# Batch 0 laid out anew in an attention-and-MoE kernel, and two 256-query tiles put into one MoE group

## The chip, the core and the metric

The kernel runs on one core of a Trainium2 chip. TensorE (PE) multiplies matrices into PSUM, VectorE (DVE), ScalarE (ACT) and GpSimd (POOL) work elementwise, and SyncE (SP) issues transfers; SP, ACT and POOL each have a DMA queue of their own. The metric is the device time in microseconds (us), the median of several runs.

## What is computed

The reference is block-sparse attention (4 batches, 8 heads, 768 positions, 64 channels a head) with a gated feed-forward layer behind it; its inputs and its output are float32.

```python
scores = scale * np.matmul(q, k.transpose(0, 1, 3, 2))
mask = np.abs(blk_i - blk_j) <= 1                       # blocks of 32 positions
mask = mask | (blk_i == 0) | (blk_j == 0) | (blk_i == n_blocks - 1) | (blk_j == n_blocks - 1)
for qb in range(n_blocks):
    for kb in sampled_blocks[qb]:                       # 3 for each block of queries
        mask[qb * block:(qb + 1) * block, kb * block:(kb + 1) * block] = True
attn = softmax(np.where(mask, scores, -1e9))
x = (attn @ v) laid out as (3072, 512)
h = x @ w_in                                            # (512, 2048)
out = (h / (1 + np.exp(-beta * h))) @ w_out             # (2048, 512)
```

## The kernel before, in words

**Pairs of heads.** All work is in float16 with float32 sums. The heads are taken two at a time: `seq` has 16 pairs, four a batch. For pair i, `load` (L105) brings k, q and v into a float32 stage, `cast` (L119) writes them as float16 into `kr`, `qr` (`k_rows`, `q_rows`) and `va`, and k and q are turned so that the channels lie on the partitions: `kT` and `qT`. In batch 0 TensorE turns them (`turn_by_pe`, L138: twelve 128x88 transposes for k and twelve for q, then a copy out of PSUM, L145); from batch 1 on the DMA does (`turn_by_dma`, L128). The mask rides along as 24 extra columns of `kr` and `qr` (`mask_columns`, `more_mask_columns`), so that a score matmul has 88 rows and adds a large negative number where nothing may be attended.

**Steps.** `unit` cuts the work of a pair and a tile of 256 or 512 queries into steps. A step is score matmuls (`sc`, L246: four of 256 columns, or two of 512) and one exponential of 128x1024 on ScalarE (`et`, L249). Some steps later come the products with v (`av`, L268: twelve or twenty-four matmuls a head), the division by the sum (`recip`, `xst`, L273 and L274), and the turn of the result into `xt` (`turn_out`: TensorE, `xtp`, L285, or the DMA, L290). There are 144 steps, 36 a batch, numbered x; steps 0 to 11 are the 256-query tile of batch 0, steps 12 to 35 its 512-query tile.

**MoE groups.** When all four pairs of a tile are in `xt`, the tile "arrives" and its feed-forward work is queued: sixteen h steps (`hp`, L307: four matmuls; tanh on ScalarE, `t_sb`, L312; the product `g` on VectorE, L314) and an o step for each half of 128 queries' output (`op`, L326: eight matmuls of 512 columns), with `osb` (L331) and a store at the end. `feed` puts a share of this queue after every step, so that TensorE has it to do while ScalarE exponentiates. The first tile arrives at step 15.

**Order.** The schedule is written by hand: each engine runs its instructions in the order of the code. The loop over x says what is put where: casts of later batches at `cast_at`, loads at `load_at`, the turns of batch 0's pairs 1 to 3 at x = 0, 3 and 6, and the casts and turns of the last four of the six columns of queries of its pairs at x = 8 to 11. All loads and stores are on SP's queue, but for the weights, which GpSimd's queue takes and casts in the transfer.

Of the kernel before, what the change touches and what calls it, by code (L numbers as in the profile page):

```python
# [17 lines left out]
def kernel(  # L18
# [78 lines left out]
    for t in va_tiles:  # L97
        nc.gpsimd.memset(t[:, :, :, D:VW], 1.0)
    for t in k_rows + q_rows:
        nc.gpsimd.memset(t[:, :, :, KR:P], 0.0)  # L100
# [3 lines left out]
    def load(i, name, c0=0, c1=NC, split=False):  # L104
# [27 lines left out]
    def turn_by_pe(i, which, c0, c1, on_act):  # L132
        rows = (k_rows, q_rows)[which][i % NST]
        dst = kq[seq[i]][which]
        for h in range(2):
            tp = mm_pool.tile([P, NC, P], FP16, tag="mm", name="tp")
            for c in range(c0, c1):
                nc.tensor.transpose(out=tp[0:KR, c, :], in_=rows[:, h, c, 0:KR],  # L138
                                    identity=identity)
            o = dst[0:KR, h, c0 * P:c1 * P]  # L140
            i_ = tp[0:KR, c0:c1, :].rearrange("p c s -> p (c s)")
            if on_act is not None and on_act == h:
# [38 lines left out]
    def mask_columns(x, first, on_act):  # L181
# [7 lines left out]
        else:  # L189
# [4 lines left out]
    id16 = persist.tile([NB, NB], FP16, name="id16")  # L194
    nc.vector.tensor_copy(out=id16, in_=ident)
# [3 lines left out]
    mask_blk = persist.tile([NB, NB], FP32, name="mask_blk")  # L199
    nc.vector.tensor_tensor(out=mask_blk, in0=dif, in1=dif, op=ALU.mult)  # L200
    nc.vector.tensor_scalar(out=mask_blk, in0=mask_blk, scalar1=1.5, scalar2=None,
                            op0=ALU.is_le)
    for val in (0.0, float(NB - 1)):
        nc.vector.scalar_tensor_tensor(out=mask_blk, in0=iota_j, scalar=val, in1=mask_blk,
                                       op0=ALU.is_equal, op1=ALU.max)
        nc.vector.scalar_tensor_tensor(
            out=mask_blk, in0=iota_i[:, 0:1].to_broadcast([NB, NB]), scalar=val,
            in1=mask_blk, op0=ALU.is_equal, op1=ALU.max)
    sb_f32 = persist.tile([NB, 3], FP32, name="sb_f32")
    nc.vector.tensor_copy(out=sb_f32, in_=sb_i32)  # L210
    mask_columns(id16, k_rows[0], True)
    keep_warm(9)
    for r in range(3):
        nc.vector.scalar_tensor_tensor(out=mask_blk, in0=iota_j, scalar=sb_f32[:, r:r + 1],
                                       in1=mask_blk, op0=ALU.is_equal, op1=ALU.max)
    mask16 = persist.tile([NB, NB], FP16, name="mask16")
    nc.vector.tensor_scalar(out=mask16, in0=mask_blk, scalar1=1.0, scalar2=-NEG,
                            op0=ALU.subtract, op1=ALU.mult)
# [16 lines left out]
    def unit(b, j, q0, n, group, by_pe):  # L235
# [44 lines left out]
        def turn_out():  # L280
                xst, xt = box["x"], xt_tiles[group]
                if by_pe:
# [4 lines left out]
                    nc.vector.tensor_copy(out=xt[:, j, 0:n],  # L287
                                          in_=xtp[:, 0:nq, :].rearrange("p c s -> p (c s)"))
                else:
                    nc.sync.dma_start_transpose(  # L290
                        out=xt[:, j, 0:n].rearrange("p (c s) -> p c s", s=P),
# [5 lines left out]
    def moe_steps(group, b, q0, n):  # L297
        box = {}

        def h_step(f):  # L300
            def run():
# [3 lines left out]
                hp = mm_pool.tile([P, 512], FP32, tag="mm", name="hp")  # L305
# [13 lines left out]
        def o_step(ts, half):  # L319
            def run():  # L320
# [8 lines left out]
                if half == 1:  # L329
                    osb = work_pool.tile([P, D_MODEL], FP32, tag="osb", name="osb")  # L330
                    nc.vector.tensor_scalar(out=osb, in0=op, scalar1=0.5, scalar2=None,  # L331
                                            op0=ALU.mult)
                    rows = out[b * S:(b + 1) * S, :].rearrange("(p c) m -> c p m", c=NC)
                    nc.sync.dma_start(out=rows[q0 // P + ts], in_=osb)
# [156 lines left out]
```

## Time and profile before

| | |
|---|---|
| median of 3 runs | 311.38 us (309.2 to 312.13) |
| profiled execution | 311.44 us |
| its span, first to last instruction | 309.5 us |
| mean granted TensorE clock | 0.975 |
| busy: PE / ACT / DVE / POOL | 289.8 / 208.6 / 155.8 / 17.6 us |
| moved by DMA | 41.30 MB |

A busy matmul in the profile is not one at its peak, since matmuls are pipelined and their ends are modelled. So the pace of matmuls is read from stretches in which many follow one another.

### The profile page before, as it was taken

Reading aid. Unit: us, or ns where it says so; the run is one execution under the profiler, and the core shown is the slowest. Engines: PE = TensorE matmul, PEld = TensorE weight load, DVE = VectorE, ACT = ScalarE, POOL = GpSimd, SP = SyncE. Lnnn points to the kernel's source line nnn. Section 1 sums busy time; section 2 is a strip of 40 time slices with the busy share of each in tenths; the row PEclk is TensorE's granted clock in tenths of the full one; section 3 lists DMA queues with packets and bytes.
Section 4 is the critical chain, followed back from the end, with each engine's and each line's share of the span. In section 5 each row is a group of like instructions: output and inputs, shape, how many; then the busy total and the mean of one; then the engine's idle time right before and its main releaser. Section 6 shows DMA issues by size and latency. Waiting matters only on the chain.

```text
span 309.5 us, 6342 instructions
## 1 busy us (share of the span) xinstructions
PE 289.8 (94%) x2588; PEld 175.9 (57%) x2588; DVE 155.8 (50%) x383; ACT 208.6 (67%) x277; POOL 17.6 (6%) x40
## 2 busy tenths in 40 slices
PE   7876999889999998999999999999999999999894
PEld 5755576445555554656666656655555565554651
DVE  6765357543576442664426446624554126752551
ACT  3553599757997555996658778868996558850350
POOL 7680000000000000000000000000000000000000
PEclk9995599999999999999999999999999999999999
DMA  5999997996348989303362969551000210001101
GB/s 170 341 257 245 267 185 182 280 230 180 85 153 103 306 223 222 70 10 112 124 208 58 241 132 271 102 128 36 18 19 0 87 53 34 0 2 68 70 0 68
DMA packets 68447, 41.30 MB, mean 133 GB/s; under 512 B 47924, under 2 KB 65348, under 8 KB 68420
## 3 DMA queue, kind: packets, MB, share of 16 engines
q1 hardware_dynamic: 64196, 36.72, 46.5%
q0 software_dynamic: 4224, 4.19, 8.2%
q8 instruction: 20, 0.33, 0.4%
q14 instruction: 7, 0.06, 0.0%
HBM read 27.27 MB, written 6.29 MB: 108 GB/s over the span
## 4 chain that ended last, share of the span: by engine, by line
PE 81%; DVE 8%; ACT 6%; issue 3%; DMA 1%; ACTq 0%; DVEq 0%
PE op L326 27%; PE hp L307 22%; PE sc L246 18%; PE av L268 11%; ACT t_sb L312 4%; PE tp L138 2%; ACT et L249 2%; DVE g L314 2%; DMA xt<-xst 1%; DVE qr L119 1%; DVE kT L145 1%; DVE xst L274 1%; DVE osb L331 0%; DVE recip L273 0%; PE xtp L285 0%
## 5 line engine op out<-in xcount | busy, mean ns | idle before, releaser
L249 ACT ACTIVATE et<-sc 128x1024 f16<-128x1024 f32 x144 | 145.4, 1026 | 60.4 <-PE sc L246 60.4
L307 PE MATMUL hp<-xt,w_in_sb 128*128 128x256 f16 (+1 forms) x512 | 97.1, 326 | 5.8 <-DVE g L314 2.8
L314 DVE SCALAR_TENSOR_TENSOR g<-t_sb,hp 128x256 f16<-128x256 f16 (+1 forms) x128 | 70.1, 554 | 62.5 <-ACT t_sb L312 62.3
L312 ACT ACTIVATE t_sb<-hp,beta_h_sb 128x256 f16<-128x256 f32 (+1 forms) x128 | 73.0, 586 | 25.3 <-PE hp L307 24.1
L246 PE MATMUL sc<-qT,kT 88*128 88x256 f16 (+1 forms) x384 | 87.3, 335 | 2.8 <-ACT et L249 2.6
L326 PE MATMUL op<-w_out_sb,g 128*128 128x512 f16 x384 | 89.7, 379 | 0.0
L307 PEld LDWEIGHTS <-w_in_sb 128*128 128x128 f16 x512 | 47.9, 97 | 39.8 <-issue 8.3
L326 PEld LDWEIGHTS <-g 128*128 128x128 f16 x384 | 36.0, 97 | 38.8
L246 PEld LDWEIGHTS <-kT 88*128 88x128 f16 x384 | 37.3, 100 | 26.2 <-issue 3.9
L268 PEld LDWEIGHTS <-et 128*128 128x128 f16 x1152 | 45.9, 99 | 11.0 <-DVE xst L274 1.5
L268 PE MATMUL av<-va,et 128*128 128x65 f16 x1152 | 48.2, 195 | 0.3 <-DVE xst L274 0.3
L331 DVE TENSOR_SCALAR osb<-op 128x512 f32<-128x512 f32 x24 | 16.6, 691 | 35.7 <-PE op L326 35.7
L273 DVE RECIPROCAL recip<-av 128x2 f32<-128x2 f32 (+1 forms) x64 | 11.1, 173 | 39.0 <-PE av L268 38.5
L274 DVE TENSOR_TENSOR xst<-av,recip 128x128 f16<-128x128 f32 (+1 forms) x64 | 22.9, 358 | 2.2
L119 DVE CAST qr<-qst 128x768 f16<-128x768 f32 (+2 forms) x20 | 10.7, 533 | 0.3 <-DMA qst<-in_q_dram 0.3
L138 PE MATMUL tp<-identity,qr 128*88 128x128 f16 x48 | 6.1, 272 | 4.2 <-DVE qr L119 3.8
L138 PEld LDWEIGHTS <-qr 128*88 128x88 f16 x48 | 4.6, 157 | 5.1 <-DVE qr L119 4.4
L119 DVE CAST kr<-kst 128x768 f16<-128x768 f32 x13 | 7.4, 572 | 0.0
L119 DVE CAST va<-vst 128x768 f16<-128x768 f32 x12 | 6.6, 554 | 0.9 <-DMA vst<-in_v_dram 0.9
L145 DVE COPY qT<-tp 88x256 f16<-88x256 f16 (+1 forms) x16 | 5.1, 348 | 2.5 <-PE tp L138 2.5
L145 DVE COPY kT<-tp 88x768 f16<-88x768 f16 x7 | 3.7, 551 | 3.1 <-PE tp L138 3.0
L287 DVE COPY xt<-xtp 128x256 f16<-128x256 f16 (+1 forms) x12 | 4.0, 333 | 2.1 <-PE xtp L285 1.9
(47 smaller groups left out, 50.8 us busy)
## 6 DMA issues: line engine op xcount, KB each, us to landing
vst<-in_v_dram SPq DMA_DIRECT2D x16, 384.0 KB, 4.8
out_dram<-osb SPq DMA_DIRECT2D x24, 256.0 KB, 2.1
kst<-in_k_dram SPq DMA_DIRECT2D x15, 384.0 KB, 4.0
qst<-in_q_dram SPq DMA_DIRECT2D x12, 384.0 KB, 4.5
w_in_sb<-in_moe_w_in_dram POOLq DMA_DIRECT2D x4, 512.0 KB, 10.7
w_out_sb<-in_moe_w_out_dram POOLq DMA_DIRECT2D x4, 512.0 KB, 22.7
qst<-in_q_dram SPq DMA_DIRECT2D x4, 256.0 KB, 6.9
qst<-in_q_dram SPq DMA_DIRECT2D x4, 128.0 KB, 4.2
```

Of the source, the lines that this page charges most:

```text
L119: eng.tensor_copy(out=dst[:, :, c0:c1, 0:D], in_=st[:, :, c0:c1, :])
L138: nc.tensor.transpose(out=tp[0:KR, c, :], in_=rows[:, h, c, 0:KR], identity=identity)
L145: nc.vector.tensor_copy(out=o, in_=i_)
L246: nc.tensor.matmul(sc[:, i, :], lhsT=kT[0:KR, hh, kc * P:(kc + 1) * P], rhs=qT[0:KR, hh, q0:q0 + n], start=True, stop=True)
L249: nc.scalar.activation(out=et, in_=sc, func=AF.Exp, bias=0.0, scale=SCALE)
L268: nc.tensor.matmul(at[:, qc, :], lhsT=ets[(hh, kc)][:, qc * P:(qc + 1) * P], rhs=va[:, hh, kc, 0:D + 1], start=(kc == 0), stop=(kc == NC - 1))
L274: nc.vector.tensor_tensor(out=xst[:, 0:nq, hh * D:(hh + 1) * D], in0=at[:, 0:nq, 0:D], in1=recip[:, 0:nq].to_broadcast([P, nq, D]), op=ALU ...
L307: nc.tensor.matmul(hp[:, 0:n], lhsT=w_in_sb[:, c, f * P:(f + 1) * P], rhs=xt[:, c, 0:n], start=(c == 0), stop=(c == NPAIR - 1))
L312: nc.scalar.activation(out=t_sb[:, 0:n], in_=hp[:, 0:n], func=AF.Tanh, bias=0.0, scale=beta_h_sb[:, f:f + 1])
L314: nc.vector.scalar_tensor_tensor(out=g[:, f, 0:n], in0=t_sb[:, 0:n], scalar=1.0, in1=hp[:, 0:n], op0=ALU.add, op1=ALU.mult)
L326: nc.tensor.matmul(op, lhsT=g[:, f, ts * P:(ts + 1) * P], rhs=w_out_sb[:, f, :], start=(f == 0), stop=(f == N_FFC - 1))
L331: nc.vector.tensor_scalar(out=osb, in0=op, scalar1=0.5, scalar2=None, op0=ALU.mult)
```

## The change

It is in five places.

- **Queues at the start.** The load of the sampled blocks, of the first q and of beta go to ScalarE's queue. The mask is built in fewer VectorE steps. The first k is cast and turned one head at a time.
- **Batch 0.** `turn_by_pe` takes one head; a pair's k is turned at x = 0, 3, 6 and the first part of its q one step later. The later q columns are cast on GpSimd ahead of time, and turned at x = 9 to 12. The copies of the mask columns go from VectorE to GpSimd. The clearing of the rows' padding moves behind the weights.
- **Batch 1.** Its loads go to GpSimd's queue, for its first pair (pair 4) between and behind the weights. Pair 4 is turned by TensorE at x = 30 to 33.
- **Casts.** All casts of batches 1 to 3 go from VectorE to GpSimd.
- **MoE.** The 256-query tiles of batches 1 and 2 form one group of 512. The last pair of every group is turned by TensorE, and a group arrives four steps after its last scores (before, six where the DMA turned it). The last group's h steps take every third PSUM buffer from the score pool.

```diff
-    nc.sync.dma_start(out=sb_i32, in_=sb_lo)
+    nc.scalar.dma_start(out=sb_i32, in_=sb_lo)
...
-    load(0, "q", 0, 2)
-    nc.sync.dma_start(out=beta_sb, in_=moe_beta.rearrange("(c p) -> c p", p=P))
+    load(0, "q", 0, 2, eng=nc.scalar)
     load(1, "k")
...
     def more_mask_columns(i):
         for rows in (k_rows, q_rows):
-            nc.vector.tensor_copy(out=rows[i][:, :, :, D:KR], in_=rows[0][:, :, :, D:KR])
+            nc.gpsimd.tensor_copy(out=rows[i][:, :, :, D:KR], in_=rows[0][:, :, :, D:KR])
...
+    groups = [[(0, 0, 256)], [(0, 256, 512)], [(1, 0, 512)], [(1, 512, 256), (2, 0, 256)],
+              [(2, 256, 512)], [(3, 0, 512)], [(3, 512, 256)]]
...
-                hp = mm_pool.tile([P, 512], FP32, tag="mm", name="hp")
+                if group == last and f % 3 == 2:
+                    hp = sc_pool.tile([P, 2, 512], FP32, tag="sc", name="hps")[:, 0, :]
+                else:
+                    hp = mm_pool.tile([P, 512], FP32, tag="mm", name="hp")
...
-        by_pe = ti < 2 or ti == len(tiles) - 1
+                by_pe = gi < 2 or gi == last or j == NPAIR - 1
...
-        arrivals.append(e + (4 if by_pe else 6))
+        arrivals.append(e + 4)
...
+    load_w_in(2)
+    load_w_in(3)
+    for i in range(NPAIR):
+        cast(i, "q", nc.gpsimd, 2, NC)
+    load(4, "k", eng=nc.gpsimd)
+    load(4, "q", eng=nc.gpsimd)
     for i in range(4):
         load_w_out(i)
+    load(4, "v", eng=nc.gpsimd)
+    for t in k_rows + q_rows:
+        nc.gpsimd.memset(t[:, :, :, KR:P], 0.0)
-    load_at = dict(zip(range(4, 16), (14, 17, 20, 24, 38, 44, 50, 56, 76, 82, 88, 94)))
-    cast_at = dict(zip(range(4, 16), (21, 25, 28, 32, 48, 53, 57, 63, 86, 92, 98, 104)))
+    load_at = dict(zip(range(4, 16), (20, 22, 30, 35, 38, 44, 50, 56, 76, 82, 88, 94)))
+    cast_at = dict(zip(range(4, 16), (29, 33, 36, 40, 48, 53, 57, 63, 86, 92, 98, 104)))
...
-        if x in (0, 3, 6):
+        if x < 9:
             i = x // 3 + 1
-            more_mask_columns(i)
-            cast(i, "q", nc.vector, 0, 2)
-            turn_by_pe(i, 0, 0, NC, None)
-            turn_by_pe(i, 1, 0, 2, None)
+            if x % 3 == 0:
+                cast(i, "q", nc.vector, 0, 2)
+                turn_by_pe(i, 0, 0, 0, NC, ((0, NC, False),))
+                turn_by_pe(i, 0, 1, 0, NC, ((0, NC, False),))
+            if x % 3 == 1:
+                turn_by_pe(i, 1, 0, 0, 2, ((0, 2, False),))
+                turn_by_pe(i, 1, 1, 0, 2, ((0, 2, False),))
...
-        if x in (8, 9, 10, 11):
-            cast(x - 8, "q", nc.vector, 2, NC)
-            turn_by_pe(x - 8, 1, 2, NC, None)
+        if 9 <= x < 13:
+            for h in range(2):
+                turn_by_pe(x - 9, 1, h, 2, NC, ((2, NC, False),))
         for i in range(NPAIR, len(seq)):
             if load_at[i] == x:
                 for name in "kqv":
-                    load(i, name)
+                    if i > NPAIR:
+                        load(i, name, eng=nc.gpsimd if i < 2 * NPAIR else nc.sync)
             if cast_at[i] == x:
                 for name in "kqv":
-                    cast(i, name, nc.vector)
+                    cast(i, name, nc.gpsimd)
...
-            if cast_at[i] + 2 == x:
+            if cast_at[i] + 2 == x and i > NPAIR:
                 turn_by_dma(i)
+        if 30 <= x < 34:
+            turn_by_pe(NPAIR, x % 2, (x - 30) // 2, 0, NC, ((0, NC, False),))
```

VectorE's queue at steps 8 to 11, before: `qr` is the float16 copy of q, `tp` the turned one in PSUM.

```order
L119 CAST qr_103<-qst 128x2x4x64
L145 COPY qT<-tp 88x512 x2
L287 COPY xt<-xtp 128x256
L119 CAST qr_104<-qst 128x2x4x64
L145 COPY qT<-tp 88x512 x2
L273 RECIPROCAL recip<-av 128x2
L274 TENSOR_TENSOR xst<-av,recip 128x2x64
L119 CAST qr_105<-qst 128x2x4x64
L145 COPY qT<-tp 88x512 x2
```

The same place with the change, at steps 9 to 12:

```order
L138 COPY qT<-tp 88x512 x2
L272 RECIPROCAL recip<-av 128x2
L273 TENSOR_TENSOR xst<-av,recip 128x2x64
L138 COPY qT<-tp 88x512 x2
L272 RECIPROCAL recip<-av 128x2
L273 TENSOR_TENSOR xst<-av,recip 128x2x64
L138 COPY qT<-tp 88x512 x2
```

The casts have left VectorE's queue. On GpSimd's queue, where before only the last v casts and then the eight weight transfers stood, they now stand here:

```order
L111 CAST va_107<-vst 128x12x64
L146 DMA w_in_sb<-in_moe_w_in_dram 128x4x512 x2
L111 CAST qr_100<-qst 128x2x4x64
L111 CAST qr_101<-qst 128x2x4x64
L111 CAST qr_102<-qst 128x2x4x64
L111 CAST qr_103<-qst 128x2x4x64
L105 DMA kst<-in_k_dram 128x2x384
L105 DMA qst<-in_q_dram 128x2x384
L150 DMA w_out_sb<-in_moe_w_out_dram 128x4x512 x4
L105 DMA vst<-in_v_dram 128x2x384
```

They stand behind all v casts and the four transfers of w_in, and pair 4's k and q are loaded ahead of w_out, its v behind it. Further on, GpSimd's queue casts pair 4, and between that and the next pair's casts stand the next loads (`waits` names the semaphore that an instruction waits for: DMASW ones are raised by transfers of GpSimd's own queue, and there are eight):

```order
L111 CAST va_108<-vst 128x12x64 [waits DMASW2_49]
L105 DMA kst<-in_k_dram 128x2x384 [waits DMASW6_49,Pool_49]
L105 DMA qst<-in_q_dram 128x2x384 [waits DMASW7_49,DVE_49]
L105 DMA vst<-in_v_dram 128x2x384 [waits DMASW0_49,Pool_49]
L111 CAST kr_97<-kst 128x12x64 [waits DMASW3_49]
```

Pair 4's v cast thus stands ahead of pair 6's loads and of pair 5's casts, and from the ninth transfer on, a transfer waits until the one eight places before it has landed.

## Rows read from the trace of the kernel before

**Rows 1.** Stretches (us): PE, PEld, DVE, ACT, POOL busy (instructions), granted clock, DMA, GB/s.

```profile
20.40:24.40 4.00, 1.94 (x29) 1.50 (x29) 2.63 (x8) 2.07 (x3) 2.42 (x4) 1.00 1.23 203
24.40:38.20 13.80, 11.96 (x97) 8.24 (x98) 5.77 (x19) 5.99 (x7) 0.00 (x0) 0.51 1.16 261
38.20:56.00 17.80, 16.14 (x191) 11.68 (x190) 11.46 (x31) 16.78 (x28) 0.00 (x0) 1.00 0.98 196
...
73.75:290.20 216.45, 212.98 (x1860) 123.91 (x1859) 105.84 (x241) 154.92 (x202) 0.00 (x0) 1.00 0.44 108
```

**Rows 2.** Chain of waits, pieces in order of time: start, us, engine, tile, line.

```profile
96.43 0.76 PE av L268 x24
97.19 1.73 PE op L326 x8
98.92 0.86 PE sc L246 x4
...
172.30 0.87 PE hp L307 x8
```

**Rows 3.** ScalarE in order of time: start, us, what, count, [idle before and its end].

```profile
9.54 1.02 ACT L249 ACTIVATE et<-sc 128x1024 f16<-128x1024 f32 x1 [1.69 <-PE sc L246]
11.63 2.85 ACT L249 ACTIVATE et<-sc 128x1024 f16<-128x1024 f32 x3 [1.07 <-PE sc L246]
...
19.70 1.94 ACT L249 ACTIVATE et<-sc 128x1024 f16<-128x1024 f32 x2 [1.68 <-PE sc L246]
...
37.52 1.02 ACT L249 ACTIVATE et<-sc 128x1024 f16<-128x1024 f32 x1 [0.49 <-PE sc L246]
...
56.03 1.94 ACT L249 ACTIVATE et<-sc 128x1024 f16<-128x1024 f32 x2
```

**Rows 4.** Who waited for whom: us in total, times, longest.

```profile
PE tp L138 <- DVE qr L119: 3.8, 4, 1.2
POOL va L119 <- DMA vst<-in_v_dram: 2.8, 4, 0.9
```

**Rows 5.** All engines in order of time, batch 0; SPq is SP's queue issuing.

```profile
0.74 1.00 SPq L79 DMA_DIRECT2D sb_i<-in_sampled_blocks_dram  x1
...
4.74 0.47 SPq L113 DMA_DIRECT2D vst<-in_v_dram  x1
...
11.88 0.86 POOL L119 CAST va<-vst 128x768 f16<-128x768 f32 x1 [0.65 <-DMA vst<-in_v_dram]
11.97 0.91 DVE L119 CAST qr<-qst 128x256 f16<-128x256 f32 x1
...
13.14 0.83 PE L138 MATMUL tp<-identity,kr 128*88 128x128 f16 x12
...
15.95 0.83 POOL L119 CAST va<-vst 128x768 f16<-128x768 f32 x1 [0.70 <-DMA vst<-in_v_dram]
16.72 3.14 POOL L153 DMA_DIRECT2D w_in_sb<-in_moe_w_in_dram  x4
...
17.58 0.22 DVE L119 CAST qr<-qst 128x256 f16<-128x256 f32 x1
```

**Rows 6.** DMA issues: KB each, median us from issue to landing.

```profile
vst<-in_v_dram SPq DMA_DIRECT2D x16, 384.0 KB, 4.8
...
w_out_sb<-in_moe_w_out_dram POOLq DMA_DIRECT2D x4, 512.0 KB, 22.7
qst<-in_q_dram SPq DMA_DIRECT2D x4, 256.0 KB, 6.9
...
qT<-qr SPq DMA_TRANSPOSE x12, 4.6
```

**Rows 7.** TensorE in order of time, [idle before and its end].

```profile
121.82 1.24 PE L307 MATMUL hp<-xt,w_in_sb 128*128 128x512 f16 x5 [1.45 <-DMA xt<-xst]
...
194.57 0.60 PE L307 MATMUL hp<-xt,w_in_sb 128*128 128x256 f16 x4 [0.57 <-DVE g L314]
...
290.21 8.34 PE L307 MATMUL hp<-xt,w_in_sb 128*128 128x256 f16 x61 [0.54 <-DVE xt L287]
```

More of the change, by code (lines that the diff above doesn't have):

```diff
@@ L96, with load @@
     make_identity(nc, identity)
[L97 to L100, printed above, removed]
     loaded, kq = {}, {}
-    def load(i, name, c0=0, c1=NC, split=False):
+    def load(i, name, c0=0, c1=NC, split=False, eng=nc.sync):
         b, j = seq[i]
@@ L130, in turn_by_dma, with turn_by_pe @@
                 in_=rows.rearrange("p h c s -> p (h c s)"))
-    def turn_by_pe(i, which, c0, c1, on_act):
+    def turn_by_pe(i, which, h, c0, c1, evac):
         rows = (k_rows, q_rows)[which][i % NST]
         dst = kq[seq[i]][which]
[L135 to L142, printed above, removed]
+        tp = mm_pool.tile([P, NC, P], FP16, tag="mm", name="tp")
+        for c in range(c0, c1):
+            nc.tensor.transpose(out=tp[0:KR, c, :], in_=rows[:, h, c, 0:KR],
+                                identity=identity)
+        for a, z, on_act in evac:
+            o = dst[0:KR, h, a * P:z * P]
+            i_ = tp[0:KR, a:z, :].rearrange("p c s -> p (c s)")
+            if on_act:
                 nc.scalar.activation(out=o, in_=i_, func=AF.Copy, bias=0.0, scale=1.0)
@@ L206 @@
         nc.vector.scalar_tensor_tensor(
[L207 to L210, printed above, removed]
+            out=far, in0=iota_i[:, 0:1].to_broadcast([NB, NB]), scalar=val,
+            in1=far, op0=ALU.not_equal, op1=ALU.min)
     mask_columns(id16, k_rows[0], True)
     keep_warm(9)
-    for r in range(3):
-        nc.vector.scalar_tensor_tensor(out=mask_blk, in0=iota_j, scalar=sb_f32[:, r:r + 1],
-                                       in1=mask_blk, op0=ALU.is_equal, op1=ALU.max)
+    cast(0, "k", nc.vector, h0=0, h1=1)
@@ L233, with unit @@
     xt_tiles = {}
-    def unit(b, j, q0, n, group, by_pe):
+    def unit(b, j, q0, n, group, at0, by_pe):
         kn = 1024 // n
@@ L290, in turn_out, with moe_steps @@
                     nc.sync.dma_start_transpose(
-                        out=xt[:, j, 0:n].rearrange("p (c s) -> p c s", s=P),
+                        out=xt[:, j, at0:at0 + n].rearrange("p (c s) -> p c s", s=P),
                         in_=xst[:, 0:nq, :].rearrange("p c s -> p (c s)"))
         return steps, [av(0), av(1), turn_out]
-    def moe_steps(group, b, q0, n):
+    groups = [[(0, 0, 256)], [(0, 256, 512)], [(1, 0, 512)], [(1, 512, 256), (2, 0, 256)],
+              [(2, 256, 512)], [(3, 0, 512)], [(3, 512, 256)]]
+    last = len(groups) - 1
+    def moe_steps(group):
         box = {}
+        chunks = [(b, q0 // P + c) for b, q0, n in groups[group] for c in range(n // P)]
+        n = P * len(chunks)
         def h_step(f):
@@ L332, in run @@
                                             op0=ALU.mult)
+                    b, c = chunks[ts]
                     rows = out[b * S:(b + 1) * S, :].rearrange("(p c) m -> c p m", c=NC)
-                    nc.sync.dma_start(out=rows[q0 // P + ts], in_=osb)
+                    nc.sync.dma_start(out=rows[c], in_=osb)
             return run
@@ L360 @@
     flip = [0]
-    todo = sum(t[2] for t in tiles) * 128 / 2400.0
+    todo = B * S * 128 / 2400.0
     def choose(want_h):
```

105 lines of the change are left out of this document (60 added, 45 removed).

## Prediction

> **What bounds the kernel now.** I began with the table of stretches, then took the pace of matmuls from the chain of waits, and then followed ScalarE, GpSimd and TensorE in order of time. In steady stretches TensorE is the bound: eight o-step matmuls of 512 columns take 1.73 us, four score matmuls of 512 or eight of 256 take 0.86, eight h matmuls of 256 take 0.87, and 24 products with v take 0.76 [rows 2]. At this pace the work that the code gives TensorE between 73.75 and 290.20 us is 105 steps of scores at 0.43 (45.2), h matmuls worth 320 of 512 columns at 0.216 (69.1; the 64 others belong to the first and the last group), 320 op matmuls (69.1) and 864 av matmuls at 0.0317 (27.4): 210.8 of 216.45 us [rows 1]. So only some 5.6 us can be won in the two thirds of the kernel that look full.
>
> The start is different. Step 0's exponential begins at 9.54 us, step 1's at 11.63, step 7's at 19.70, step 15's at 37.52, step 27's at 56.03 [rows 3]. From steps 1 to 8 a step takes (19.70 + 0.97 - 11.63) / 7 = 1.29 us. From step 8 (20.67) to step 15 seven steps take 16.85 us, 2.41 each, though the exponential takes 0.97 when several follow one another (1.94 for two). Two things are to be seen there. TensorE waits four times for a VectorE cast of q that stands just ahead of its turn, 3.8 us in all [rows 4]. And TensorE's clock falls: in 20.40 to 24.40 us it was busy for 1.94 of 4.00 us, and in 24.40 to 38.20 the granted clock was 0.51, the 1.2 GHz level [rows 1]. From step 15 to 27 ScalarE is the bound, busy 16.78 of 17.80 us [rows 1], at (56.03 - 37.52) / 12 = 1.54 us a step.
>
> **The change, part by part** (against the profiled execution: span 309.5 us, time 311.44, so 1.94 around the span; its time is within 0.1 us of the median, 311.38).
>
> *Start: -0.8 us.* The sampled blocks, first q and beta leave SP's queue, so the first k is issued where the blocks were, their 1.00 us earlier [rows 5]. ScalarE now issues three transfers before it loads its table; that is beside k's landing. Step 1 is not freed by as much: pair 1's turn now waits for mask columns that GpSimd copies behind pair 0's v cast. v0's issue moves from 4.74 us by the three issues that leave (1.00 and two like its own 0.47 [rows 5]) to 2.8; 4.8 to land [rows 6], 0.83 to cast, and two copies of 288 columns on GpSimd, which no row shows (between 0.22, a VectorE cast of 256, and 0.83, GpSimd's cast of 768; I take 0.4, by columns nearer the first), make about 9.2; then 12 turns at the early pace, the scores, and step 1's exponential at some 10.8 instead of 11.63. Bounds: 0 and -1.5.
>
> *Steps 1 to 8: -0.6.* The mask copies go from VectorE, a pair's k and q are turned in different steps, and no copy stands ahead of a turn. Per three steps TensorE has 1.29 of scores, 0.87 of turns (16 at 0.83/12 [rows 5], pipelined 0.054), 0.76 of av and 0.1: 3.0 us, and ScalarE 2.91. I take 1.2 us a step, not the 1.0 of a perfect fit, since VectorE's copies out of PSUM must fit in too. Bounds: 0 and 7 x (1.29 - 0.97) = -2.2.
>
> *Steps 8 to 15: -7.7.* The four casts are done on GpSimd beforehand. Will they be in time? GpSimd's last v cast ended at 16.78 [rows 5], and it had waited 2.8 us for v alone [rows 4], which covers the six mask copies (2.4); of the four w_in issues at 3.14/4 two are taken as hidden in its other waits, and two bring 18.4; the casts (two thirds of 0.83) then end at 19.0 to 20.6. Step 9's turn falls due at about 19.5, and the later q takes 6.9 us to land [rows 6] behind the last v's issue, so I allow 0.8 for one wait. Steps 9 to 12 have on TensorE 0.43 + 8 turns (0.43) + 0.38: 1.3 each; steps 13 to 15 are ScalarE's, 1.05 each. 4 x 1.3 + 3 x 1.05 + 0.8 = 9.15 instead of 16.85. Bounds: 7 exponentials at 0.97 = 6.8 (-10.0), and the old stretch at half clock without its waits, 16.85 - 3.8 = 13.1 (-3.8). I am nearer the first, since the clock fell after TensorE had waited and the waits go; whether it falls all the same is a rival below.
>
> *Steps 15 to 27: -0.8.* ScalarE idled 17.80 - 16.78 = 1.0 us [rows 1], mostly behind VectorE's casts of batch 1, which leave. Bounds: 0 and -1.0.
>
> *Steps 27 to 39: +0.5.* Pair 4's 24 turns come onto TensorE, 24 x 0.054 = 1.3 us; some fall where TensorE waits for an exponential. Bounds: 0 and +1.3. That batch 1's other casts leave VectorE I cost at nothing: TensorE and ScalarE set the pace there.
>
> *Batch 1's data: 0.* w_in, pair 4's k and q, w_out and pair 4's v pass one queue, and GpSimd stops in pair 4's v cast until w_out and v have landed. Issued at about 23 us, w_out would land near 46 at its 22.7 us [rows 6], the v about 48. Behind it GpSimd casts it (0.83), issues pair 6's loads (3 x 0.79) and casts pair 5 (3 x 0.83), to 54; two DMA turns at 4.6 [rows 6] end at 63. Pair 5's scores, step 42, are due near 46 + 15 x 1.54 = 69. The cover is 6 us; the second rival is its loss.
>
> *xt: -1.4.* The 1.45 us wait for an xt that the DMA turned [rows 7] goes, since the last pair of every group is now turned by TensorE.
>
> *Merge: -2.5.* In the 256-query groups TensorE waits for VectorE's g, one wait of 0.57 us as an example [rows 7], and the scores behind it on its queue wait too. Of the 5.6 us above, 1.4 is xt; of the 4.2 left I take some 60%. Bounds: -0.6, the one wait, and -4.2.
>
> *Tail: -1.0.* The 61 h matmuls from 290.21 take 8.34 us [rows 7]; at 0.87 for eight they are 6.6. Two more PSUM buffers let TensorE run ahead of g. Bounds: 0 and -1.7; I take 1.0, since ScalarE's sixteen tanhs must keep up. The o step and store behind it are as before.
>
> Sum: -0.8 - 0.6 - 7.7 - 0.8 + 0.5 - 1.4 - 2.5 - 1.0 = **-14.3**: span 295.2, time **297.1 us**.
>
> **A row and a rule.** VectorE's cast of 128x256 took 0.91 us at 11.97, beside a GpSimd cast from 11.88 to 12.74, and 0.22 at 17.58 with none beside it [rows 5]. Three such casts stay on VectorE, at steps 0, 3 and 6, while GpSimd gets more to do: if each is held so, 3 x 0.69 = 2.1 us. The Trainium skill ("SBUF — State Buffer", Who interferes with whom) says that VectorE and GpSimd share a port pair as an exclusive lock, so the later one blocks for the other's whole instruction; by that the sum would be -12.2, and that speaks against moving casts to GpSimd. The trace agrees for that cast. Most of VectorE's later work reads PSUM, and the rows show no such stretching there.
>
> **Rivals.**
> 1. *The clock falls again* (0.20). Steps 13 to 15 give TensorE 0.43 + 0.25 of work in 1.05 us, little more than the half it had before the fall [rows 1]. For it: that share. Against: 9 to 12 are full and h steps follow at once. At half clock a step of the first group costs TensorE (0.43 + 0.25 + 0.58) x 2 = 2.5 instead of 1.47 us; over 6 us, under half of the old 13.8, that loses 6 x (1 - 1.47 / 2.5) = 2.5, and 1 more goes in steps 13 to 15: 301 us.
> 2. *GpSimd's queue holds batch 1 up* (0.05): slower. If w_out, which now has pair 4's k and q ahead of it, lands D later than the 46 us above, GpSimd stops for D in pair 4's v cast, with pair 6's loads and pair 5's casts behind it; step 42 waits D - 6. It decides from D = 6 on; the 14.3 are lost at D = 20, and at D = 24, a landing of 47 us instead of 22.7, the time is 297.1 + 18 = 315. Against: the transfers put ahead are two loads, and such loads took 4.8 to 6.9 on SP [rows 6].
> 3. *The change doesn't move the stall off TensorE* (0.18): GpSimd's casts are late or VectorE's are held as in the rule above, so steps 1 to 12 gain 2 to 3 us less: 299.5.
> 4. *Everything fits better* (0.07): steps 8 to 15 at ScalarE's pace (2.3 more), the whole merge gain (1.7), steps 1 to 8 at 1.05 (1.0): 292.
> 5. *Eaten* (0.05): the early steps win 5 us less, and 6 us are lost again in waits for weights or for pair 5 (D = 12): 308.
>
> The forecast itself has 0.45, with its own range 294 to 299.5.
>
> **Numbers.** Predicted 297.1 us. The range, 290.5 to 304, holds the forecast, rivals 1, 3 and 4 and the bounds of the early steps, and leaves out 2 and 5 and tails. Within 1% (308.3 to 314.5), about what a measurement can tell from no change, and slower take rivals 5 and 2 and a little of 1 each: faster by over 1% 0.88, within 1% 0.07, slower 0.05.
>
> **What the profile after would show.** Right: step 15's exponential near 28.5 us, step 27's near 46; no TensorE wait for a q cast; a granted clock of 1.00 from 20 to 40 us; no wait of hp for a DMA-turned xt; tail h steps of about 7.3 us. Wrong: a clock of 0.5 after 25 us (rival 1), GpSimd idle behind a transfer while TensorE waits for a kT or qT at step 42 or 48 (rival 2), turns waiting for GpSimd at step 9, VectorE casts of 0.9 us (rival 3). The forecast fails above all if steps 8 to 15 do not close up, since more than half of it is there.

## The result, and the profile after

The changed kernel takes 300.28 us (median of 4 runs, 299.71 to 300.76), the kernel before 311.06 (4 runs, 309.2 to 312.13): a ratio of 0.966, interval 0.961 to 0.971. Predicted were 297.1 us, in a range of 290.5 to 304. The profiled execution took 300.59 us, its span is 298.8 (before: 309.5).

The time can be cut into eight stretches at points that both traces have: the starts of five exponentials, the last group's last turn, and the start of the last group's o steps.

| from ... to | before | after | difference | predicted |
|---|---|---|---|---|
| first instruction ... step 1 | 11.63 | 11.62 | 0.0 | -0.8 |
| step 1 ... step 8 | 8.99 | 8.73 | -0.3 | -0.6 |
| step 8 ... step 15 | 16.90 | 8.42 | -8.5 | -7.7 |
| step 15 ... step 27 | 18.51 | 17.58 | -0.9 | -0.8 |
| step 27 ... step 38 | 17.34 | 17.74 | +0.4 | +0.5 |
| step 38 ... last group's turn | 215.75 | 216.72 | **+1.0** | **-3.9** (xt -1.4, merge -2.5) |
| last turn ... last group's o steps | 9.27 | 7.26 | -2.0 | -1.0 |
| last group's o steps ... end | 11.09 | 10.74 | -0.4 | 0 |
| sum | 309.5 | 298.8 | -10.7 | -14.3 |

So the early steps came about as predicted, and the long middle part, where 3.9 us were to be won, became 1 us longer. First the stretches of the changed kernel, to be held beside [rows 1] (columns as there: length, busy time and instructions of PE, PEld, DVE, ACT, POOL, granted clock, DMA share, GB/s):

```profile
8.00:12.00 4.00, 3.92 (x31) 3.04 (x30) 2.14 (x7) 1.90 (x3) 3.61 (x13) 0.57 0.82 236
12.00:20.35 8.35, 6.65 (x98) 5.44 (x95) 6.35 (x19) 6.53 (x7) 7.88 (x13) 1.00 1.10 293
20.35:28.77 8.42, 7.91 (x117) 5.75 (x117) 5.77 (x22) 7.06 (x7) 7.20 (x12) 1.00 1.23 226
28.77:46.35 17.58, 16.81 (x195) 12.18 (x196) 9.28 (x27) 17.41 (x29) 9.53 (x17) 1.00 1.08 249
...
64.09:280.75 216.66, 214.18 (x1812) 117.77 (x1809) 94.69 (x206) 153.17 (x186) 19.85 (x24) 1.00 0.46 113
```

The third row is steps 8 to 15: the clock column, 0.51 in [rows 1], is 1.00, and TensorE is busy for 7.91 of 8.42 us. In the fourth, ScalarE is busy for 17.41 of 17.58. In the last, TensorE is busy for 214.18 of 216.66 us, more than the 212.98 of 216.45 before: it was given work there, not relieved. ScalarE in order of time, beside [rows 3]:

```profile
9.17 1.02 ACT L248 ACTIVATE et<-sc 128x1024 f16<-128x1024 f32 x1 [0.42 <-PE sc L245]
11.62 6.03 ACT L248 ACTIVATE et<-sc 128x1024 f16<-128x1024 f32 x6 [1.42 <-PE sc L245]
17.84 1.02 ACT L248 ACTIVATE et<-sc 128x1024 f16<-128x1024 f32 x1 [0.20 <-PE sc L245]
20.35 1.02 ACT L248 ACTIVATE et<-sc 128x1024 f16<-128x1024 f32 x1 [1.49 <-PE sc L245]
...
26.82 2.98 ACT L248 ACTIVATE et<-sc 128x1024 f16<-128x1024 f32 x3 [0.37 <-PE sc L245]
...
46.35 1.02 ACT L248 ACTIVATE et<-sc 128x1024 f16<-128x1024 f32 x1
```

Steps 1 to 6 follow one another without a gap, and then 1.49 us are idle ahead of step 8. What TensorE waits for, beside [rows 4]:

```profile
PE xtp L284 <- DVE xst L273: 1.9, 5, 0.8
PE tp L130 <- DVE qr L111: 1.5, 1, 1.5
...
PE tp L130 <- DVE kT L138: 1.1, 2, 1.0
PE av L267 <- DVE xst L273: 0.8, 5, 0.2
PE hp L316 <- DVE g L323: 0.7, 2, 0.3
```

The four waits for q casts of steps 8 to 11 are gone (the one of 1.5 us is the first q at the start). No h matmul waits for an xt from the DMA any more. In its place stand waits of the turns (`xtp`) for `xst`; experiment 6 shows what the turns cost the middle part.

### The profile page after: what moved, and what is told of

It is laid out like the page before. It is cut to its first block, busy times and chain, and to the rows that moved or that the text cites. A ratio compares the mean times of both kernels' runs of the same rounds, so it can differ in the third digit from the quotient of the medians.

```text
span 298.8 us, 6282 instructions
## 1 busy us (share of the span) xinstructions
PE 285.5 (96%) x2563; PEld 167.1 (56%) x2563; DVE 137.1 (46%) x329; ACT 206.2 (69%) x262; POOL 59.1 (20%) x98
## 4 chain that ended last, share of the span: by engine, by line
PE 84%; DVE 5%; ACT 4%; issue 2%; DMA 2%; SPq 1%; POOL 0%; ACTq 0%
PE op L335 28%; PE hp L316 25%; PE sc L245 17%; PE av L267 12%; ACT t_sb L321 2%; ACT et L248 2%; DMA vst<-in_v_dram 2%; PE tp L130 2%; DVE xst L273 2%; PE xtp L284 1%; DVE recip L272 1%; PE hps L316 1%; DVE kT L138 1%; DVE g L323 1%; SPq L105 1%
## 5 line engine op out<-in xcount | busy, mean ns | idle before, releaser
L316 PE MATMUL hp<-xt,w_in_sb 128*128 128x512 f16 (+1 forms) x428 | 92.9, 351 | 0.8 <-DVE g L323 0.7
L323 DVE SCALAR_TENSOR_TENSOR g<-t_sb,hp 128x512 f16<-128x512 f16 (+1 forms) x107 | 65.9, 620 | 53.3 <-ACT t_sb L321 53.0
L321 ACT ACTIVATE t_sb<-hp,beta_h_sb 128x512 f16<-128x512 f32 (+1 forms) x107 | 67.1, 638 | 17.8 <-PE hp L316 16.6
L316 PEld LDWEIGHTS <-w_in_sb 128*128 128x128 f16 x448 | 41.5, 97 | 34.5 <-issue 1.3
L111 POOL CAST kr<-kst 128x768 f16<-128x768 f32 x15 | 12.4, 828 | 96.8 <-DMA kst<-in_k_dram 96.8
L111 POOL CAST va<-vst 128x768 f16<-128x768 f32 x16 | 13.2, 827 | 16.1 <-DMA vst<-in_v_dram 14.2
L111 POOL CAST qr<-qst 128x768 f16<-128x768 f32 (+1 forms) x16 | 12.2, 777 | 2.1 <-DMA qst<-in_q_dram 1.4
L138 DVE COPY kT<-tp 88x768 f16<-88x768 f16 (+1 forms) x10 | 4.9, 509 | 6.5 <-PE tp L130 4.2
L284 PE MATMUL xtp<-identity,xst 128*128 128x128 f16 x48 | 5.6, 221 | 2.0 <-DVE xst L273 1.9
L286 DVE COPY xt<-xtp 128x256 f16<-128x256 f16 (+1 forms) x17 | 5.8, 342 | 2.6 <-PE xtp L284 2.6
L284 PEld LDWEIGHTS <-xst 128*128 128x128 f16 x48 | 3.3, 97 | 6.0 <-DVE xst L273 4.9
```

Source lines behind the costliest of these rows:

```text
L111: eng.tensor_copy(out=dst[:, h0:h1, c0:c1, 0:D], in_=st[:, h0:h1, c0:c1, :])
L284: nc.tensor.transpose(out=xtp[:, qc, :], in_=xst[:, qc, :], identity=identity)
L316: nc.tensor.matmul(hp[:, 0:n], lhsT=w_in_sb[:, c, f * P:(f + 1) * P], rhs=xt[:, c, 0:n], start=(c == 0), stop=(c == NPAIR - 1))
L321: nc.scalar.activation(out=t_sb[:, 0:n], in_=hp[:, 0:n], func=AF.Tanh, bias=0.0, scale=beta_h_sb[:, f:f + 1])
L323: nc.vector.scalar_tensor_tensor(out=g[:, f, 0:n], in0=t_sb[:, 0:n], scalar=1.0, in1=hp[:, 0:n], op0=ALU.add, op1=ALU.mult)
```

## The experiments

The kernel before ran in turn with each group of experiments, and its own runs differ. On one chip four of its eleven runs had a mean granted clock of 0.993 or more and took 306.7 to 308.6 us; the seven others, at 0.971 to 0.986, took 308.8 to 313.4. The changed kernel ran again beside experiments 5, 10 and 12 (it is experiment 11); where another experiment is held against it, the chip is another, and the stretches of the traces count for more than the times. Times are medians of six runs, in experiments 3 and 4 of twelve. **In these experiments "later casts" are the four q casts of [rows 4].**

**1. Only the casts moved.** The kernel before, with the four later casts put on GpSimd behind the w_in transfers, nothing else.

```diff
+    for i in range(NPAIR):
+        cast(i, "q", nc.gpsimd, 2, NC)
...
-            cast(x - 8, "q", nc.vector, 2, NC)
```

> The kernel before (311 us) with one part of the change alone: its four later q casts go to GpSimd, behind the four issues of w_in and ahead of w_out's. My theory: most of the largest term comes by this alone: steps 8 to 15 take 9 to 11 us instead of 16.85, granted clock 1.00, time 303 to 306 us. Rival: it needs the per-head turns and GpSimd's other relief too: the clock still falls, at most 4 us less, 307 or more.

303.43 us (303.04 to 306.06), against 308.25 (306.82 to 311.4) of the kernel before on that chip; ratio 0.982, interval 0.977 to 0.988. Its stretch of steps 8 to 15:

```profile
20.28:28.32 8.04, 7.91 (x117) 5.97 (x117) 5.54 (x21) 6.86 (x8) 4.52 (x7) 1.00 1.19 237
```

8.04 us at a clock of 1.00: these casts alone close the stretch that the whole change closes to 8.42. The per-head turns add nothing to that. Against the eight runs of the kernel before on that chip whose mean clock was 0.994 or more (306.8 to 308.2 us, mean 307.5), the casts alone gain 4.0 us.

**2. The casts put back.** The changed kernel, with the later casts on VectorE ahead of their turns.

```diff
-    for i in range(NPAIR):
-        cast(i, "q", nc.gpsimd, 2, NC)
...
         if 9 <= x < 13:
+            cast(x - 9, "q", nc.vector, 2, NC)
```

> The four later casts of q go back from GpSimd to VectorE, each just ahead of its turn at steps 9 to 12; all else as in the changed kernel (300.3 us). My theory: the wait for the cast and the clock that falls after it were the largest term, so steps 8 to 15 take 13 to 16.8 us again instead of 8.4, the granted clock is near 0.5 for some 10 us after 22 us, and the time is 305 to 308 us. Rival: the waits alone cost, the clock fell for the sparse start before them: clock 1.00, some 3.5 us more, 304.

308.84 us (303.48 to 309.35). Five of the six runs, at a mean clock of 0.976 to 0.987, took 308.7 to 309.4; the sixth, at 0.999, took 303.48, the rival's time. The five lost more than four waits are worth. VectorE and GpSimd in order of time (start, length, what, count):

```profile
28.13 4.23 DVE L111 CAST qr<-qst 128x512 f16<-128x512 f32 x1
```
```profile
27.79 0.71 POOL L105 DMA_DIRECT2D vst<-in_v_dram  x1 [1.64 <-DMA w_in_sb<-in_moe_w_in_dram]
28.49 1.83 POOL L432 MEMSET kr<- 128x480 f16 x4
30.25 1.84 POOL L432 MEMSET qr<- 128x480 f16 x4
```

The fourth cast, alone some 0.42 us, stood through a transfer's issue and eight clearings on GpSimd, and ended 0.27 us behind the last of them. (The second cast, at 23.54 us, lay inside the issue of another transfer, 23.32 to 24.26, and took 0.42: an issue doesn't always hold one.) TensorE's turns:

```profile
26.43 0.64 PE L130 MATMUL tp<-identity,qr 128*88 128x128 f16 x8 [0.95 <-DVE qr L111]
...
32.42 1.08 PE L130 MATMUL tp<-identity,qr 128*88 128x128 f16 x8 [4.54 <-DVE qr L111]
```

After three waits, of 0.72, 0.92 and 0.95 us, the third turn still took 0.64 us; the clock was 1.00 to 28 us and fell around the wait of 4.54 (0.62 in 28 to 32 us). So this run mixed two things, and the two that follow it were made to part them.

**3. The same, with TensorE kept busy** by seven matmuls on zeros of 256 columns ahead of each of the four turns.

```diff
         if 9 <= x < 13:
             cast(x - 9, "q", nc.vector, 2, NC)
+            wps = mm_pool.tile([P, 512], FP32, tag="mm", name="fill")
+            for _ in range(7):
+                nc.tensor.matmul(wps[:, 0:256], lhsT=zeros[:, 0:P], rhs=zeros[:, 0:256],
+                                 start=True, stop=True)
```

> As the run with the q casts on VectorE, but seven matmuls of 256 columns on zeros (0.76 us) stand on TensorE ahead of each of the four turns, where it would wait for the cast. My theory: the idle time let the clock fall, so it stays at 1.00 and only the delay of the turns is left: 301 to 304 us. Rival: the clock falls all the same, and the time is that of the run without the filling, or above.

308.59 us (303.57 to 310.56). The clock was 1.00 through the first three casts, to 28 us, but so it was in experiment 2 without the filling; then the fourth cast was held for 4.17 us beside the same clearings, and the clock fell all the same (0.87 in 28 to 32 us, 0.50 in 32 to 36). Three of the twelve runs, at a mean clock of 0.994 to 1.000, took 303.6 to 304.2 us, as the theory had it; the nine others, at 0.978 to 0.989, took 307.5 to 310.6. Inconclusive, for the reason of experiment 2.

**4. The same as 2, with the clearings put at step 20 in the code.**

```diff
-    for t in k_rows + q_rows:
-        nc.gpsimd.memset(t[:, :, :, KR:P], 0.0)
...
+        if x == 20:
+            for t in k_rows + q_rows:
+                nc.gpsimd.memset(t[:, :, :, KR:P], 0.0)
```

> The changed kernel with the four later q casts put back on VectorE just ahead of their turns, and with GpSimd's eight clearings of the row padding moved from behind the weights to step 20, so that no GpSimd work stands beside the fourth cast. Theory A (the casts in VectorE's queue cost TensorE about one microsecond each, and it was the clearings beside the fourth cast that held it 4.2 us and let the clock fall): four waits of 0.7 to 1.0 us for q, fourth cast under 1.2 us, granted clock 1.00 in 28 to 36 us, time 303 to 304.5. Theory B (waits for q by themselves make the clock fall, whatever stands on GpSimd): granted clock near 0.5 for some 8 to 13 us behind the waits, time 306 to 309.

309.32 us (308.57 to 310.99). The edit missed: GpSimd runs in order, no other work of its queue stands between the old place and the new one, and the clearings ran at 29.35, behind the same transfers, and held the fourth cast for 3.21 us. But one thing is to be seen: the clock was 0.94 in 24 to 28 us and 0.50 from 28 on, so it had fallen before the held cast began (30.02), after three plain waits.

**5. The same as 2, with the clearings behind pair 5's casts.**

```diff
-        if x == 20:
+        if x == 34:
```

> The changed kernel with the four later q casts back on VectorE just ahead of their turns; the eight clearings of the row padding stand on GpSimd behind the casts of pair 5 (step 34), so that between GpSimd's last v cast and pair 4's casts only transfer issues stand on its queue, and pair 4's own k and q casts behind them. Theory A (held casts made the loss): no VectorE cast over 1 us at steps 9 to 12, the fourth wait of TensorE under 1.2 us, granted clock 1.00 throughout, time 302.5 to 304.5, that is 2 to 4 above the changed kernel. Theory B (waits of 0.7 to 0.9 us one after another let the clock fall by themselves): the waits as in A, but the clock at 0.5 for some 8 us from about 27 us on, time 305 to 308. If the fourth cast is held all the same, by pair 4's casts: over 1 us beside a GpSimd cast, and the time as in B.

305.67 us (303.7 to 306.7); the changed kernel beside it, experiment 11, 300.57. No cast at steps 9 to 12 takes over 0.42 us. TensorE in order of time, and the stretches:

```profile
21.66 0.64 PE L130 MATMUL tp<-identity,qr 128*88 128x128 f16 x8 [0.71 <-DVE qr L111]
...
24.05 0.64 PE L130 MATMUL tp<-identity,qr 128*88 128x128 f16 x8 [0.92 <-DVE qr L111]
...
26.43 1.08 PE L130 MATMUL tp<-identity,qr 128*88 128x128 f16 x8 [0.92 <-DVE qr L111]
...
29.62 1.08 PE L130 MATMUL tp<-identity,qr 128*88 128x128 f16 x8 [0.72 <-DVE qr L111]
```
```profile
20.00:24.00 4.00, 2.26 (x33) 1.60 (x29) 2.63 (x9) 2.48 (x3) 2.62 (x4) 1.00 1.24 204
24.00:28.00 4.00, 3.03 (x34) 2.31 (x34) 2.39 (x7) 1.02 (x1) 1.92 (x4) 0.78 1.26 214
28.00:32.00 4.00, 3.28 (x26) 2.14 (x26) 1.64 (x5) 1.37 (x2) 1.69 (x3) 0.50 1.13 299
```

The same eight turns take 0.64 us, 0.64 and then 1.08: the clock fell between the second turn and the third, with no held cast near. So theory B holds for the profiled run. In two of the six runs the mean clock was 0.994 and 1.000, and these took 303.7 and 304.26 us, theory A's time; the four others, at 0.981 to 0.992, took 305.6 to 306.7. Both happen: the waits cost some 3.4 us (304.0 - 300.57), and the fall that follows them in most runs 1.6 to 2.7 more. That the held cast costs another 3 to 3.6 us (308.6 to 309.3 in experiments 2 to 4 against 305.67) is not shown: those ran on other chips, and their runs at a clock of 0.994 or more took 303.5 to 304.2 us, no longer than such runs here. Nor does the fall follow each time: in experiment 2 three like waits had passed without it.

**6. The DMA turns the last pair of the middle groups again**, and such a group arrives six steps after its last scores, as before.

```diff
-                by_pe = gi < 2 or gi == last or j == NPAIR - 1
+                by_pe = gi < 2 or gi == last
...
-        arrivals.append(e + 4)
+        arrivals.append(e + (4 if by_pe else 6))
```

> The changed kernel with xt as before: the DMA turns the last pair of the middle groups too, and these arrive six steps after their scores. My theory, formed from the two traces: each turn on TensorE costs 0.22 us of work and some 0.46 us of waiting for xst ahead of it, so four of them cost 2.7 us and took back what the vanished wait of 1.45 us gave: time 298 to 300 us, TensorE at the pace of its matmuls where xtp stood. Rival, the prediction's term: the wait for the DMA comes back once or oftener, and it is 1.4 us or more slower, 301.7.

297.34 us (296.81 to 298.29), 2.9 less than the changed kernel on another chip. From step 38 to the last turn it takes 213.28 us, where the changed kernel takes 216.72 and the one before 215.75. TensorE's groups in 64 to 281 us, first of the changed kernel, then of this one (busy us, mean ns | idle ahead, and what ended it):

```profile
L316 PE MATMUL hp<-xt,w_in_sb 128*128 128x512 f16 x322 | 78.2, 378 | 0.1
...
L267 PE MATMUL av<-va,et 128*128 128x65 f16 x864 | 35.2, 193 | 0.6 <-DVE xst L273 0.3
L284 PE MATMUL xtp<-identity,xst 128*128 128x128 f16 x28 | 3.2, 220 | 1.7 <-DVE xst L273 1.7
```
```profile
L316 PE MATMUL hp<-xt,w_in_sb 128*128 128x512 f16 (+1 forms) x344 | 81.3, 371 | 1.8 <-DMA xt<-xst 1.0 <-DVE xt L286 0.5
...
L267 PE MATMUL av<-va,et 128*128 128x65 f16 x864 | 35.1, 193 | 0.0
L284 PE MATMUL xtp<-identity,xst 128*128 128x128 f16 x8 | 1.1, 219 | 0.0
```

The turns on TensorE bring their own matmuls (16 for the four middle groups, 0.9 us at 0.054; 4 more of the 28 belong to batch 0 and lie just inside the window) and wait for VectorE's `xst` just ahead of them, while the DMA's turn waits for nothing on TensorE's queue. One such wait:

```profile
106.94 0.40 PE L284 MATMUL xtp<-identity,xst 128*128 128x128 f16 x4 [0.29 <-DVE xst L273]
```

The wait for a DMA-turned xt, 1.45 us in [rows 7], is 1.04 here, once. The 0.5 us for `xt` L286 in its rows lies behind the last turn. So idle time and matmuls in these rows explain 2.0 of the 3.4 us (16 more turns, 0.9, and 2.4 against 1.3 us idle); the rest is in gaps that the modelled ends hide. From the start of each matmul to the start of the next, over the same stretch, the scores take 2.7 us less than in the changed kernel, the products with v 1.0 and the turns 0.9 less, the h matmuls 1.2 more. Not parted: the turn and the arrival were changed together.

**7. The two 256-query tiles as two groups again**, in the changed kernel.

```diff
-    groups = [..., [(1, 512, 256), (2, 0, 256)],
+    groups = [..., [(1, 512, 256)], [(2, 0, 256)],
```

> The changed kernel with the two 256-query tiles of batches 1 and 2 as two groups again, all else kept. If the merge is worth what the prediction took (2.5 us): 302.0 to 303.5, with waits of 256-column h matmuls for g back in the trace. If the merge removes the waits but gives the time back as av matmuls waiting for xst in the 256-query tiles (the accounting of the changed kernel's trace): within 0.8 us of the changed kernel, 300 to 301. If the merge costs: below 299.7.

301.6 us (301.2 to 302.44). Step 38 to the last turn is 217.88 us, 1.16 more than in the changed kernel, and the waits of hp for g grow from 0.7 to 1.6 us. Between the two theories: the merge gives 1.2 us, less than 2.5, more than nothing. Counted from start to start as above, it takes 2.3 us from the h matmuls and gives 1.4 back to the scores.

**8. The last group without the score-pool buffers.**

```diff
-                if group == last and f % 3 == 2:
+                if False:
```

> The changed kernel without the score-pool buffers in the last group's h steps; all else kept. Prediction's tail term (1.0 us comes from these buffers): last group's 61 h matmuls near 8.2 to 8.4 us instead of 7.2, time 301.0 to 301.6. Rival (the tail is shorter only because the last pair's turn and the group's arrival differ): h matmuls stay at 7.2 to 7.4, time 300 to 300.6.

301.19 us (301.01 to 302.56). The last group's h steps:

```profile
279.93 8.89 PE L316 MATMUL hp<-xt,w_in_sb 128*128 128x256 f16 x64
288.66 7.07 PE L335 MATMUL op<-w_out_sb,g 128*128 128x512 f16 x32
```

From the turn's start (279.87) to 288.66 are 8.79 us, 7.26 in the changed kernel: the buffers give 1.5, as the term said, a little more. In this trace an early accident (experiment 9) had not happened, which hides some of it in the sum.

**9. The start.** First q ahead of the sampled blocks on ScalarE's queue, pair 1's mask columns ahead of pair 0's v cast, the first q casts of pairs 1 to 3 on GpSimd.

```diff
-    nc.scalar.dma_start(out=sb_i32, in_=sb_lo)
...
     load(0, "q", 0, 2, eng=nc.scalar)
+    nc.scalar.dma_start(out=sb_i32, in_=sb_lo)
...
+    more_mask_columns(1)
+    cast(1, "q", nc.gpsimd, 0, 2)
     nc.gpsimd.memset(va_tiles[0][:, :, :, D:VW], 1.0)
...
-                cast(i, "q", nc.vector, 0, 2)
```

> The changed kernel with three things moved at the start: the first q is issued ahead of the sampled blocks on ScalarE's queue, pair 1's mask columns are copied on GpSimd ahead of pair 0's v cast, and the first q casts of pairs 1 to 3 are done on GpSimd behind each pair's mask columns instead of on VectorE. Theory (the start term failed because pair 1's turn waited for the mask copy behind the v cast, and step 8 was late by a VectorE cast held 1.66 us beside GpSimd): step 1's exponential at 10.3 to 11.0 instead of 11.62, step 8's near 18.6 instead of 20.35, no VectorE cast over 1 us in steps 0 to 8, time 298.0 to 299.2. Rival (GpSimd then becomes late with v or with the later q, or the early half clock sets the pace): step 15 no earlier than 28.4, time 299.8 to 301.

299.67 us (299.17 to 300.05). Step 1 begins at 10.62 us, step 8 at 18.56, step 15 at 27.07: 1.0, 1.8 and 1.7 earlier. The three moves were not parted. The theory's cause, the mask copy, is not the first one, as GpSimd and TensorE of the changed kernel show:

```profile
7.97 0.82 POOL L111 CAST va<-vst 128x768 f16<-128x768 f32 x1 [0.82 <-DMA vst<-in_v_dram]
8.74 0.43 POOL L221 COPY kr<-kr 128x288 f16<-128x288 f16 x1
```
```profile
7.50 0.39 PE L130 MATMUL tp<-identity,qr 128*88 128x128 f16 x4 [1.54 <-DVE qr L111]
7.72 0.50 PE L130 MATMUL tp<-identity,kr 128*88 128x128 f16 x6
8.15 0.98 PE L245 MATMUL sc<-qT,kT 88*128 88x256 f16 x4
9.22 1.51 PE L130 MATMUL tp<-identity,kr 128*88 128x128 f16 x12
10.52 1.06 PE L245 MATMUL sc<-qT,kT 88*128 88x256 f16 x4
```

Pair 1's k is turned at 9.22 us, just behind this copy, but step 0's scores, ahead of it on TensorE, ended only at 9.13: the copy cost at most 0.09 us. Ahead of them it had waited 1.54 us for the cast of the first q, which ScalarE's queue issues behind the sampled blocks; the first turn of k, at 5.05, was 1.1 us earlier than before. With both moved, pair 1's turn begins at 8.68. The median is 0.6 to 0.9 lower, on another chip. A part of the profile's 1.7 us is an accident of the profiled run of the changed kernel: step 7 to 8 took 2.51 us in it and 2.44 in experiment 11, but 1.31 to 1.37 in experiments 6, 7 and 8, whose start is the same. There VectorE's cast was held once more:

```profile
16.42 0.75 POOL L146 DMA_DIRECT2D w_in_sb<-in_moe_w_in_dram  x1
16.59 1.66 DVE L111 CAST qr<-qst 128x256 f16<-128x256 f32 x1
...
17.16 0.83 POOL L111 CAST va<-vst 128x768 f16<-128x768 f32 x1
```

In experiment 6 the same cast took 0.40 us, in experiment 7 0.28, though there too it began during a transfer's issue (0.11 us behind its start, here 0.17). What decides it is not shown.

**10. All casts of batches 1 to 3 back on VectorE.**

```diff
-                    cast(i, name, nc.gpsimd)
+                    cast(i, name, nc.vector)
```

> The changed kernel with the casts of all of batches 1 to 3 back on VectorE; the queues of their loads, and all else, kept. Prediction's term (0.8 us in steps 15 to 27, nothing later): step 27's exponential 0.5 to 1.0 us later than the changed kernel's 46.35, time 0.5 to 1.2 us longer. Rival (VectorE has room everywhere): within 0.4 us. Other rival (casts on GpSimd hold VectorE's work on SBUF, so that taking them back helps the later stretches): up to 1 us shorter.

300.14 us (299.54 to 301.59), beside 300.57 of the changed kernel: no difference. Steps 15 to 27 take 17.56 us (17.58 there), steps 27 to 38 17.75 (17.74). The engine of these casts is worth nothing.

**11. The changed kernel again**, unedited, and **12. all that gained**: experiment 9's diff and the first line of experiment 6's, with an arrival after seven steps in place of six.

```diff
-        arrivals.append(e + 4)
+        arrivals.append(e + (4 if by_pe else 7))
```

> The changed kernel itself, on the chip of the other kernels of this call, so that they can be compared with it: 299.7 to 300.8.

> The changed kernel with the three early moves (first q ahead of the sampled blocks on ScalarE's queue, pair 1's mask columns ahead of pair 0's v cast, first q casts of pairs 1 to 3 on GpSimd), and with the last pair of the middle groups turned by the DMA again, such a group arriving seven steps after its last scores. If the gains add: the early moves 0.6 to 1.4 us and the DMA turn 2.5 to 3 us below the changed kernel on the same chip, 296 to 297; with the remaining 1.0 us wait for a DMA-turned xt gone as well, 295 to 296. Rival (the early gain is lost in the end or a group's work comes too late at seven steps): 297 to 298.5.

300.57 us (299.38 to 301.82) and 298.31 (297.08 to 298.62): 2.3 less, but 1.0 more than experiment 6 alone, which ran on another chip. The gains did not add. Step 15 is early (27.02), but from step 38 to the last turn it takes 214.15 us, 0.9 more than at six steps, though the wait for a DMA-turned xt is down to 0.50: with the later arrival, 13.19 us of work are left from the last exponential to the last turn, 11.47 at six steps. The start's moves with six steps were not run.

## Why the prediction was right, and where it was not

The measured 300.28 us lies in the stated range, but 3.2 us above the forecast and outside the forecast's own 294 to 299.5. The signs that it named as right came (step 15 at 28.77 us for 28.5, step 27 at 46.35 for 46, no wait for a later q cast, clock 1.00 behind 12 us, 7.26 us for the tail's h steps for 7.3). But for the vanished wait for `xt`, none of them watched the long middle part, which missed by 4.9 us; the other stretches together gave 1.2 us more than forecast, so the sum is nearer than its parts.

- **Steps 8 to 15 (-7.7; -8.5): right, with its mechanism.** Experiment 1 shows that the moved casts do it. But the size rests on which execution was profiled: the stretch at half clock is not in every run of the kernel before. By experiment 5 the waits alone are worth some 3.4 us (by experiment 1, 4.0), and the runs of the kernel before at a lower clock are on average 3.5 longer (311.2 against 307.7); 1.0 to 1.6 of the 8.5 us are not accounted for. Against runs of the kernel before with a clock of 0.993 or more the changed kernel on the same chip gains 7.1 us, not 10.7.
- **xt (-1.4): the step that failed.** The wait that it named is gone. What "is now turned by TensorE" itself costs was set at nothing: 16 matmuls, and a wait for `xst` ahead of each group of them. Experiment 6 puts the edit, with its arrival, at +3.4 us; less the 0.4 by which the DMA's wait shrank without it, the term is +3.0. Its miss of 4.4 is more than the sum's, 3.2 us against the median: steps 8 to 15, the tail and the end gave more than their terms.
- **Merge (-2.5): the mechanism is right, the size was too large beside the turns.** 1.2 us with TensorE's turns (experiment 7). With the DMA's an estimate is 2.1, from 215.75 - 213.28 less the 0.4 by which the xt wait shrank, if nothing else counts there; no run shows it. The prediction took 60% of all the time that it could not account for; of waits for g, the kernel before has this much in the middle part:

```profile
PE hp L307 <- DVE g L314: 1.2, 2, 0.6
```

- **Start (-0.8; 0.0): failed.** The prediction put the end of the mask copies at 9.2 us and step 1 at 10.8. The first copy, k's, ended at 9.17, but from pair 1's turn at 9.22 to step 1 it took 2.40 us, 1.30 to the start of the scores and 1.10 from there, where 1.6 were allowed. And most of what k gained at the front, the wait of 1.54 us for the first q took back (experiment 9), to which the prediction gave no cost. The clock of 0.57 in 8 to 12 us does not explain it: twelve such turns took 1.48 us in the kernel before at 1.00, 1.51 here.
- **Steps 1 to 8 (-0.6; -0.3): near by two misses.** Steps 1 to 7 took 1.04 us each, better than the 1.2 that was forecast, and a held VectorE cast took some 1.2 us back ahead of step 8 (experiment 9).
- **Steps 15 to 27 (-0.8; -0.9): right in size, its reason half right.** The casts of batch 1 did leave these steps, but by their new times; that they went to GpSimd too counts for nothing (experiment 10).
- **Pair 4's turns (+0.5; +0.4), batch 1's data (0; 0): right.** No kT or qT of pair 5 was waited for, so the second rival did not occur.
- **Tail (-1.0): right in kind**, 1.5 by experiment 8.
- **The rivals.** The first, a second fall of the clock, is in no stretch after 12 us. The third is in part true: one VectorE cast held for 1.66 us, and in the second profiled execution of the same kernel (experiment 11) two, of 0.85 and 1.58 us. The Trainium skill ("SBUF — State Buffer", Who interferes with whom) has it that VectorE's two-port casts and GpSimd exclude each other for a whole instruction. The held casts agree in kind, but experiment 2 shows one held through a transfer's issue and eight clearings, 4.23 us, not through one instruction, and another that lay inside an issue took its 0.42. The rule's own sum, -12.2, came nearer to the result than the forecast, in the main for another reason: two of the three casts took 0.28 us, the held one cost 1.4 of the rule's 2.1, and the larger miss is xt. In experiment 11 held casts cost 1.9.

## What to carry to other kernels

When an edit takes a wait off an engine by giving that engine the work, price the work and the wait that comes with it: TensorE's turn needs its operand at its place in the queue, the DMA's does not. Where stalls are followed by a fall of the clock, hold the gain against undisturbed executions too, since the fall may be there in some runs only. And where casts are shared out between VectorE and GpSimd, look in the trace of both for what runs at the same moment, long rows of clearings above all.

## What the runs showed of the hardware

- A VectorE cast of 128x512 took 0.42 us with GpSimd idle (experiment 5, the fourth), and 4.23, 4.17 and 3.21 us (experiments 2 to 4) beside eight clearings of 128x480 that followed one another on GpSimd. Each time it ended 0.27 or 0.28 us behind the last of them. In each of experiments 2 to 5 the second cast lay inside the issue of a transfer on GpSimd, and took 0.42 us.
- In a row of TensorE waits of 0.7 to 0.9 us, some 2.4 us apart, the granted clock fell to 0.50 (1.2 GHz) at about the third in the profiles of experiments 4 and 5. In that of experiment 2 three such waits passed at 1.00, and two of the six runs of experiment 5 have a mean clock of 0.994 and 1.000.
- One kernel's first exponential began at 9.17 us in one profiled execution and at 10.34 in another (experiment 11), where VectorE's cast of the first q took 0.85 us beside a cast of GpSimd, 0.29 in the first; the rest of the difference is not explained. A term of under a microsecond at the start is within that.
